# Attention scores by halves of the queries on quarters of the array, and one selection for four heads

## The chip, the cores and the metric

The kernel runs on one core of a Trainium2 chip. The metric is the time of the whole program on the device, in microseconds (us). The engines are TensorE (PE for matmuls, PEld for its weight loads), VectorE (DVE), ScalarE (ACT), GpSimd (POOL) and SyncE (SP, which issues most DMAs). Matmul results land in PSUM, which VectorE and ScalarE read.

## The reference

Three layers in a row, all in fp32: windowed attention, a layer of eight experts with a capacity, and a dense layer.

```python
# q, k, v: (4, 8, 576, 64); rel[i, j] = i - j; slopes: one per head
scores = scale * np.matmul(q, k.transpose(0, 1, 3, 2))
bias = slopes[:, None, None] * (-np.abs(rel))[None, :, :]
mask = (rel >= 0) & (rel < 128)
scores = np.where(mask, scores + bias[None], -1e9)
attn = softmax(scores)                     # over the keys
x = attn @ v                               # then (2304, 512)
# experts: each token goes to one of 8, at most 288 each, by logits in sorted order
out[mask_e] = np.maximum(x[mask_e] @ w1[e], 0) @ w2[e]
# dense: h = x @ w_in; (h * sigmoid(h)) @ w_out
```

A query sees the 128 keys that end with its own, so over a block of 128 queries it needs its own block of keys and the block before.

## The kernel before

The 2304 tokens are cut into 18 tiles of 128 queries (t = 0 to 17). The heads of a tile are done in two halves of four: the first half has heads 0, 1, 4, 5, the second 2, 3, 6, 7. Heads 0 to 3 lie on partitions 0 to 63 of the loaded q and k, heads 4 to 7 on partitions 64 to 127 (j = 0, 1 in the code), so that two heads can be multiplied at once on the two row halves of the array.

Each head of a tile goes through these steps. `scores` (L196) multiplies the 128 queries of a head with 256 keys, the block before and the tile's own, into PSUM. `softmax` first selects (L217): of the two keys that stand for the same place in the block, a query keeps the one that lies in its window (the older block's where key > query, the mask `older`), for two heads at a time; since exactly 128 keys remain, everything behind works on 128 columns. L221 adds the bias table (`tab`), scales, and takes the row maximum of one head. L213 on ScalarE takes the exponential of one head. `turn` transposes the four heads of a half on TensorE (L230), ScalarE copies them out of PSUM (L238; L245 for tiles with one key block), and GpSimd splits them back into the part of the older and of the own block (L239, L241). `values` (L271) multiplies these with v, 73 columns a head, on two column halves of the array; VectorE divides by the row sums (L274 to L286). `gate` (L252) multiplies the v of the next tile with the experts' weights, on four column strips; its transpose (L259) and copy (L260) put the result beside v. `first_choices` (L83 on TensorE, L73 and L76 on GpSimd) counts experts for the routing behind attention, and from tile 4 on ScalarE and GpSimd split early expert weights (L679, L680).

Tiles 0 and 9 start a sequence with nothing before it, and have one key block (`nb` is 1). Tiles 4 and 13 hold the end of one sequence and the start of the next.

The order on TensorE, ScalarE and GpSimd is written out by hand (`keep`, `keep_in_program_order`). One turn of the loop over t runs: transposes of the tile's first half; the values of the second half of the tile before; transposes of the second half; the scores of both halves of tile t + 1; its gate; the selections, maxima and exponentials of tile t + 1; the values of the first half of tile t. In turns 1 and 2 ScalarE also scales bias tables (L352) between the two halves' exponentials. On VectorE the selections and maxima are kept in order; the divisions are placed by the scheduler between them. Scores have two buffers per head pair in PSUM, so those of one tile are written while nothing of the tile before is still read. Loads of q, k and v (L124 to L135) run three tiles ahead on SyncE's queue.

Behind attention comes the routing, a chain of short steps on VectorE and TensorE (about 120 to 150 us), and then the two expert layers and the dense layer, dense matmuls to the end.

Of the kernel before, what the change touches and what calls it, by code (L numbers as in the profile page):

```python
# [8 lines left out]
F32 = mybir.dt.float32  # L9
# [3 lines left out]
I32 = mybir.dt.int32  # L13
AF = mybir.ActivationFunctionType
ALU = mybir.AluOpType
AX = mybir.AxisListType
PSUM = bass.MemoryType.PSUM
DRAM = bass.MemoryType.DRAM

P = 128  # L20
# [9 lines left out]
def attn_consts():  # L30

    q = np.arange(P)[:, None]
    k = np.arange(P)[None, :]
    far = np.where(q >= k, q - k, q + P - k)
    first = np.where(q >= k, far, MASKED)
    upper = np.where((q >= 64) & ((k < 64) | (k > q)), MASKED, far)
    after = np.where((k < 64) & (k > q), MASKED, far)
    return np.stack([first, far, upper, after, k > q], 1).astype(np.float32)  # L40


NJ = 319
# [3 lines left out]
def first_choices(tc, at, k, X0, t, gts, pgb, room):  # L47

    nc = tc.nc
    keep = tc.keep_in_program_order  # L50
    ident, grid = k.ident, k.grid
    m = at.tile([P, 1], F32, name="m", bufs=2)
    nc.vector.tensor_reduce(m, X0[:, t, :], AX.X, ALU.min)
    if t == 0:
        yield
        pm = pgb[0:1, 0:P]
        keep(nc.tensor.transpose(pm, m, ident))
        mr = at.tile([1, 2], F32, name="mr")
        nc.vector.tensor_reduce(mr[:, 0:1], pm, AX.X, ALU.max)
        nc.vector.tensor_reduce(mr[:, 1:2], pm, AX.X, ALU.min)  # L60
        ob = at.tile([1, P], F32, name="ob")
        nc.vector.memset(ob, 1.0)
        yield
        pb = pgb[:, P:P + 2]
        keep(nc.tensor.matmul(pb, ob, mr, start=True, stop=True))
        mb = at.tile([P, 2], F32, name="mb")
        nc.vector.tensor_copy(mb, pb)
        rg = at.tile([P, 1], F32, name="rg")
        nc.vector.tensor_tensor(rg, mb[:, 0:1], mb[:, 1:2], ALU.subtract)
        nc.vector.tensor_scalar(grid, grid, rg, mb[:, 1:2], ALU.mult, ALU.add)  # L70
    yield
    fb = at.tile([P, E], BF16, name="fb", bufs=2)
    keep(nc.gpsimd.tensor_scalar(fb, X0[:, t, :], m, None, ALU.is_le))  # L73
    gt = gts[t % 2]
    if t < NT - 2:
        keep(nc.gpsimd.tensor_scalar(gt[:, 0:NJ], grid, m, None, ALU.is_le))  # L76
    else:
        keep(nc.vector.tensor_scalar(gt[:, 0:NJ].rearrange("p (a b) -> p a b", b=29),
                                     grid.rearrange("p (a b) -> p a b", b=NJ), m, None, ALU.is_le))
    yield  # L80
    if t == NT - 1:
        k.busy(tc, room, 5)
    keep(nc.tensor.matmul(pgb[0:E, 0:NJ + 1], fb, gt, start=(t == 0), stop=(t == NT - 1)))  # L83
    yield
# [6 lines left out]
def attention(ctx, tc, qT, kT, vA, vT, wg, rel, k, xtab, X0, X, pgb, wts):  # L91


    nc = tc.nc
    ident = k.ident
    at = ctx.enter_context(tc.tile_pool(name="at", bufs=1))
    ps_s = ctx.enter_context(tc.tile_pool(name="ps_s", bufs=2, space=PSUM))
    ps_t = ctx.enter_context(tc.tile_pool(name="ps_t", bufs=1, space=PSUM))
    ps_o = ctx.enter_context(tc.tile_pool(name="ps_o", bufs=2, space=PSUM))

    tab = at.tile([P, H, 4, P], F32, name="tab")
    relt = at.tile([P, 5, P], F32, name="relt")
    older = relt[:, 4:5, :].bitcast(I32).to_broadcast([P, 2, P])
    wgb = at.tile([P, 4, 32], F32, name="wgb")
    nc.gpsimd.memset(wgb, 0.0)
    ks = at.tile([P, 4, 4, P], F32, name="ks")
    va = at.tile([P, VS, H, AUG], F32, name="va")

    gts = [at.tile([P, NJ + 1], BF16, name=f"gt{i}") for i in range(2)]
# [3 lines left out]
    def slope(h):  # L113
        return -8.0 * 2.0 ** (-(h + 1))

    qs, vts = {}, {}
# [20 lines left out]
    def heads(g):  # L137
        return [2 * g, 2 * g + 1, 2 * g + 4, 2 * g + 5]

    wz = at.tile([P, 512], BF16, name="wz")  # L140
    nc.vector.memset(wz, 0.0)

    def warm(n):
        for i in range(n):
            tc.keep_in_program_order(nc.tensor.matmul(pgb, wz[:, 0:P], wz, start=True, stop=True))

    warm(10)
    load(0)
    for j in range(2):
        nc.gpsimd.dma_start(wgb[64 * j:64 * j + 64, :, 8 * j:8 * j + 8],  # L150
# [3 lines left out]
    first = at.tile([1, 1], F32, name="first")  # L154
# [11 lines left out]
    keep = tc.keep_in_program_order  # L166
    tiles, halves, gates, last = {}, {}, {}, []
# [8 lines left out]

    def open_tile(t):

        sl, ps = t % 4, (t - 1) % 4
        nb = 1 if t in (0, 9) else 2  # L180
        first, st = (sl, 1) if nb == 1 else (min(ps, sl), abs(ps - sl))
        tiles[t] = dict(nb=nb, sl=sl, ps=ps, keys=slice(first, first + (nb - 1) * st + 1, st),
                        cur=0 if nb == 1 else int(ps < sl),
                        kind=0 if nb == 1 else 2 if t in (4, 13) else 3 if t in (5, 14) else 1)

    def scores(n):
        t, g = divmod(n, 2)
        if g == 0:
            open_tile(t)
        T = tiles[t]  # L190
        pss = [ps_s.tile([P, 2, 2, P], F32, name=f"pss{j}") for j in range(2)]
        for i in range(2):
            c = 2 * g + i
            for j in range(2):
                r = slice(64 * j, 64 * j + 64)
                keep(nc.tensor.matmul(pss[j][:, i, :T["nb"], :], qs[t][r, c, :], ks[r, T["keys"], c, :], start=True, stop=True))  # L196
        halves[n] = dict(pss=pss)

    def softmax(n):
        t, g = divmod(n, 2)  # L200
        T, pss = tiles[t], halves[n]["pss"]
        cur = T["cur"]
        sc = at.tile([P, 4, P], F32, name="sc", bufs=2)
        mx = at.tile([P, 4], F32, name="mx", bufs=4)
        pe = at.tile([P, 4, P], F32, name="pe", bufs=2)
        if n == 2:
            for h in range(H):
                keep(nc.vector.tensor_scalar_mul(tab[:, h, 1, :], relt[:, 1, :], slope(h)))
        follow = []

        def exp(*cs):
            for c in cs:
                keep(nc.scalar.activation(pe[:, c, :], sc[:, c, :], AF.Exp, bias=mx[:, c:c + 1], scale=-1.0))  # L213

        for j in range(2):
            if T["nb"] == 2:
                x = nc.vector.copy_predicated(pss[j][:, :, cur, :], older, pss[j][:, :, 1 - cur, :])  # L217
                follow.append(keep(x) if follow or n > 1 else x)
            for i in range(2):
                h, c = 2 * g + 4 * j + i, 2 * j + i  # L220
                x = nc.vector.tensor_tensor_reduce(sc[:, c, :], pss[j][:, i, cur, :], tab[:, h, T["kind"], :],  # L221
                                                   -0.125, 3.0e38, ALU.add, ALU.min, mx[:, c:c + 1])
                follow.append(keep(x) if follow or n > 1 else x)
        halves[n]["pe"], halves[n]["exp"] = pe, exp

    def turn(n):
# [37 lines left out]
    def values(n):  # L264
        t, g = divmod(n, 2)
        T, parts = tiles[t], halves[n]["parts"]
        po = T["po"][g][:, 0:4 * AUG].rearrange("p (h c) -> p h c", c=AUG)
        for c in range(4):
            for i, (w, s) in enumerate(parts):
                for r in (0, 64):  # L270
                    keep(nc.tensor.matmul(po[r:r + 64, c, :], w[:, c, r:r + 64], va[:, s, heads(g)[c], :],  # L271
                                          start=(i == 0), stop=(i == len(parts) - 1), tile_position=(0, r)))
        rs = at.tile([P, 4, 1], F32, name="rs", bufs=3)
        nc.vector.tensor_scalar_add(rs, po[:, :, 72:73], 1e-9)  # L274
        nc.vector.reciprocal(rs, rs)
        nc.vector.tensor_tensor(T["lg"][:, 4 * g:4 * g + 4, :], po[:, :, D:72], rs.to_broadcast([P, 4, E]), ALU.mult)

        def x():
            return nc.vector.tensor_tensor(
                T["xt"][:, :, 2 * g:2 * g + 2, :], po[:, :, 0:D].rearrange("p (a b) d -> p a b d", a=2),  # L280
                rs.rearrange("p (a b) d -> p a b d", a=2).to_broadcast([P, 2, 2, D]), ALU.mult)

        if n < 2 * NT - 1:
            x()
        if g == 1:
            nc.vector.tensor_reduce(X0[:, t, :], T["lg"].rearrange("p h e -> p e h"), AX.X, ALU.add, negate=True)  # L286
            if t < NT - 1:
                nc.sync.dma_start(xtab[t * P:(t + 1) * P, :], T["xt"].rearrange("p a b d -> p (a b d)"))
            if t == NT - 1:
                keep(nc.gpsimd.tensor_copy(X[:, t, :], X0[:, t, :]))  # L290
            counts[t] = first_choices(tc, at, k, X0, t, gts, pgb, halves[n]["pss"][0].rearrange("p a b c -> p (a b c)"))
            next(counts[t])
            if t == NT - 1:
                last.append(x)
# [4 lines left out]
    counts = {}  # L299
# [14 lines left out]
    for t in range(NT):  # L314
        a, b = 2 * t, 2 * t + 1
# [704 lines left out]
```

## Time and profile before

| what | us |
|---|---|
| median of 3 runs (lowest to highest) | 773.82 (772.61 to 774.51) |
| profiled execution | 773.07 |
| its span, first to last instruction | 771.0 |
| TensorE busy (share of the span) | 750.1 (97%) |
| VectorE busy | 433.9 (56%) |
| ScalarE busy | 323.1 (42%) |
| GpSimd busy | 125.7 (16%) |
| scores of tile 0 start, scores of tile 17 start | 5.64, 109.99 |

Busy times overlap between engines. TensorE's matmuls are pipelined, so that its busy time says that something was in flight, not that the array worked at its full rate. Shares of the whole span mix stages with different limits: attention takes the first 120 us, the dense matmuls from about 157 us on take the rest.

### The profile page before, as it was taken

The page shows a single profiled execution, that of the slowest core. Times are in us where ns is not written, and L with a number is a line of the kernel's source. Part 1 is how long each engine was busy: PE and PEld are TensorE (multiplying, and loading weights), DVE is VectorE, ACT ScalarE, POOL GpSimd, SP SyncE. Part 2 cuts the span into 40 slices and gives each one's busy share as a digit, 9 for nine tenths or more (in the row PEclk, how much of TensorE's full clock was granted, in tenths as well). Part 3 has the DMA queues.
Part 4 walks back from the last instruction along what each step waited for, and adds up shares of the span by engine and source line. Part 5 has one row for each costly group of instructions (what it writes and reads, how often), then busy time and mean ns, then how long its engine had stood idle before and what let it go on. Part 6 is the DMA issues. An engine that isn't in the chain of part 4 may idle for free.

```text
span 771.0 us, 13966 instructions
## 1 busy us (share of the span) xinstructions
PE 750.1 (97%) x5380; PEld 643.5 (83%) x5380; DVE 433.9 (56%) x1141; ACT 323.1 (42%) x665; POOL 125.7 (16%) x183
## 2 busy tenths in 40 slices
PE   8999999699999999999999999999999999999996
PEld 5777775399999989999888888888888888888895
DVE  6888886448899768776499633222422233222331
ACT  5677772046566546554355332221412232222322
POOL 2577871321022110000000002000100001000100
PEclk9999999799999999999999999999999999999999
DMA  8999840148798688676344011000100001000100
GB/s 238 279 317 285 270 151 28 34 116 263 237 306 269 212 278 275 217 225 220 103 148 137 1 54 55 1 0 1 57 26 1 1 0 56 1 0 1 42 14 27
DMA packets 38341, 95.36 MB, mean 124 GB/s; under 512 B 4576, under 2 KB 9984, under 8 KB 38272
## 3 DMA queue, kind: packets, MB, share of 16 engines
q1 hardware_dynamic: 35072, 84.72, 34.6%
q0 software_dynamic: 3040, 9.46, 3.7%
q8 instruction: 43, 0.70, 0.4%
q10 hardware_dynamic: 160, 0.26, 0.1%
q14 instruction: 26, 0.21, 0.1%
HBM read 80.27 MB, written 14.16 MB: 122 GB/s over the span
## 4 chain that ended last, share of the span: by engine, by line
PE 64%; DMA 7%; DVE 5%; issue 2%; ACT 2%; POOLq 0%; ACTq 0%
PE y L865 25%; PE p L799 6%; DMA raw<-w 6%; PE pt L719 4%; PE p L719 4%; PE pt L720 4%; PE p L720 4%; PE pt L718 4%; PE p L718 4%; PE y L719 2%; PE y L718 2%; PE y L720 2%; DVE w L691 2%; ACT w L690 1%; PE pt L783 1%
## 5 line engine op out<-in xcount | busy, mean ns | idle before, releaser
L865 PE MATMUL y<-w,gh 128*128 128x512 f32 x548 | 180.8, 389 | 0.0
L865 PEld LDWEIGHTS y<-w,gh 128*128 128x128 f32 x548 | 102.2, 188 | 20.5
L865 PE MATMUL y<-w,gl 128*128 128x512 f32 x274 | 106.7, 389 | 0.0
L691 DVE TENSOR_TENSOR w<-raw,w 128x1024 fp32r<-128x1024 f32 x59 | 72.1, 1222 | 36.2 <-ACT w L690 36.1
L877 POOL DMA_INDIRECT out<-raw,idx x18 | 17.4, 967 | 454.5 <-ACT raw L875 420.8
L799 PE MATMUL p<-xh,w 128*128 128x288 f32 x512 | 81.1, 297 | 1.7 <-DVE hl L803 1.6
L690 ACT CAST w<-raw 128x1024 fp32r<-128x1024 f32 x59 | 61.9, 1048 | 39.8 <-DMA raw<-w 22.5
L909 DVE TENSOR_TENSOR s<-pt,s 128x512 f32<-128x512 f32 (+1 forms) x40 | 25.5, 637 | 92.3 <-ACT s L908 92.3
L909 DVE TENSOR_TENSOR s<-p,s 128x512 f32<-128x512 f32 (+1 forms) x40 | 25.5, 637 | 91.4 <-ACT s L908 91.4
L719 PE MATMUL y<-hl,w 128*128 128x288 f32 x256 | 74.4, 296 | 0.0
L799 PEld LDWEIGHTS p<-xh,w 128*128 128x128 f32 x512 | 71.6, 188 | 3.1 <-DVE hl L803 2.4
L720 PE MATMUL y<-hh,w 128*128 128x288 f32 x256 | 73.8, 295 | 0.0
L919 DVE TENSOR_TENSOR gl<-s,gh 128x512 fp32r<-128x512 f32 (+1 forms) x73 | 48.0, 658 | 42.8 <-ACT gh L918 42.7
L718 PE MATMUL y<-hh,w 128*128 128x288 f32 x256 | 69.3, 299 | 0.0
L918 ACT CAST gh<-s 128x512 fp32r<-128x512 f32 (+1 forms) x73 | 43.4, 594 | 55.3 <-DVE s L909 38.3
L908 ACT ACTIVATE s<-pt 128x512 f32<-128x512 f32 (+1 forms) x40 | 22.2, 555 | 101.8 <-PE pt L720 97.2
L908 ACT ACTIVATE s<-p 128x512 f32<-128x512 f32 (+1 forms) x40 | 22.2, 555 | 98.6 <-PE p L720 93.9
L865 PEld LDWEIGHTS y<-w,gl 128*128 128x128 f32 x274 | 51.4, 188 | 10.7
L719 PE MATMUL pt<-yl,w 128*128 128x512 f32 (+1 forms) x160 | 58.8, 368 | 0.0
L718 PE MATMUL p<-yh,w 128*128 128x512 f32 (+1 forms) x160 | 58.8, 368 | 0.0
L718 PE MATMUL pt<-yh,w 128*128 128x512 f32 (+1 forms) x160 | 58.8, 368 | 0.0
L720 PE MATMUL pt<-yh,w 128*128 128x512 f32 (+1 forms) x160 | 58.8, 368 | 0.0
(189 smaller groups left out, 1491.0 us busy)
## 6 DMA issues: line engine op xcount, KB each, us to landing
raw<-w SPq DMA_DIRECT2D x96, 512.0 KB, 4.4
va<-vA SPq DMA_DIRECT2D x18, 292.0 KB, 5.1
ks<-kT SPq DMA_DIRECT2D x36, 128.0 KB, 4.5
vt<-vT SPq DMA_DIRECT2D x18, 256.0 KB, 4.0
xtab<-xt SPq DMA_DIRECT2D x18, 256.0 KB, 5.6
yd<-yo SPq DMA_DIRECT2D x8, 576.0 KB, 4.3
qs<-qT SPq DMA_DIRECT2D x34, 128.0 KB, 4.1
yr<-yd SPq DMA_DIRECT2D x4, 1024.0 KB
```

The source lines that it names most:

```text
L690: nc.scalar.copy(hi, r)
L691: nc.vector.tensor_tensor(lo, r, hi, ALU.subtract)
L718: nc.tensor.matmul(out, whi, xhi, start=start, stop=False)
L719: nc.tensor.matmul(out, whi, xlo, start=False, stop=False)
L720: nc.tensor.matmul(out, wlo, xhi, start=False, stop=stop)
L799: nc.tensor.matmul(p, w[:, dc * P:dc * P + P], x[:, dc, :], start=(i + dc == 0), stop=(i == 2 and dc == DC - 1))
L865: mm = nc.tensor.matmul(a, x[:, w], y[:, 512:], start=(f + i == 0), stop=(f == FC2 - 1 and i == 2))
L877: nc.gpsimd.indirect_dma_start(out, bass.IndirectOffsetOnAxis(ap=idx128[:, c:c + 1], axis=0), ob, None)
L908: nc.scalar.activation(s, p, AF.Sigmoid)
L909: nc.vector.tensor_tensor(s, p, s, ALU.mult)
L918: nc.scalar.copy(gh, s)
L919: nc.vector.tensor_tensor(gl, s, gh, ALU.subtract)
```

## The change

The scores of a tile are taken by halves of the queries (u = 0: queries 0 to 63, u = 1: 64 to 127) as well as by the two row halves of the array, so that each matmul uses a quarter of the array (64 rows, 64 columns), and only the 192 keys that a half of the queries can see are multiplied. Of the older block the first half of the queries takes all 128 keys, of the own block the first 64; the second half takes the own 128 and the last 64 of the older. Keys of the older block that need no choice are written to the places of the own block that the half of the queries does not use, so that the mask for the selection is now true only within the same half of keys and queries. The selection then runs over four heads at once. The PSUM room is two fixed tiles in place of two alternating buffers, of the same size, and four of the ten starting matmuls write them once, so that nothing unwritten is read.

```diff
-    return np.stack([first, far, upper, after, k > q], 1).astype(np.float32)
+    return np.stack([first, far, upper, after, (k > q) & (k // 64 == q // 64)], 1).astype(np.float32)
...
-    older = relt[:, 4:5, :].bitcast(I32).to_broadcast([P, 2, P])
+    older = relt[:, 4:5, :].bitcast(I32).to_broadcast([P, 4, P])
...
-    warm(10)
+    warm(6)
+    banks = [ps_s.tile([P, 2, 2, 4, 64], F32, name=f"pss{i}") for i in range(2)]
+    for z in banks:
+        for j in range(2):
+            warm(1, z[:, j].rearrange("p i s x -> p (i s x)"))
...
-        pss = [ps_s.tile([P, 2, 2, P], F32, name=f"pss{j}") for j in range(2)]
+        pss = banks[n % 2]
+        sl, ps, L, R = T["sl"], T["ps"], slice(0, 64), slice(64, 128)
         for i in range(2):
             c = 2 * g + i
-            for j in range(2):
-                r = slice(64 * j, 64 * j + 64)
-                keep(nc.tensor.matmul(pss[j][:, i, :T["nb"], :], qs[t][r, c, :], ks[r, T["keys"], c, :], start=True, stop=True))
+            if T["nb"] == 2:
+                parts = [[(slice(0, 4, 3), ps, slice(0, P)), (slice(2, 4), sl, slice(0, P))],
+                         [(slice(2, 3), sl, L), (slice(1, 2), ps, R)]]
+            else:
+                parts = [[(slice(2, 4), sl, slice(0, P))] * 2]
+            for two in parts:
+                for u, (o, s, x) in enumerate(two):
+                    for j in range(2):
+                        r, m = slice(64 * j, 64 * j + 64), slice(64 * u, 64 * u + 64)
+                        keep(nc.tensor.matmul(pss[m, j, i, o], qs[t][r, c, m], ks[r, s, c, x], start=True, stop=True,
+                                              tile_position=(64 * j, 64 * u)))
...
-        for j in range(2):
-            if T["nb"] == 2:
-                x = nc.vector.copy_predicated(pss[j][:, :, cur, :], older, pss[j][:, :, 1 - cur, :])
-                follow.append(keep(x) if follow or n > 1 else x)
-            for i in range(2):
-                h, c = 2 * g + 4 * j + i, 2 * j + i
-                x = nc.vector.tensor_tensor_reduce(sc[:, c, :], pss[j][:, i, cur, :], tab[:, h, T["kind"], :],
-                                                   -0.125, 3.0e38, ALU.add, ALU.min, mx[:, c:c + 1])
-                follow.append(keep(x) if follow or n > 1 else x)
+        w = pss.rearrange("p j i (b k) x -> p (j i) b (k x)", b=2)
+        if T["nb"] == 2:
+            x = nc.vector.copy_predicated(w[:, :, 1, :], older, w[:, :, 0, :])
+            follow.append(keep(x) if n > 1 else x)
+        for c in range(4):
+            h = 2 * g + 4 * (c // 2) + c % 2
+            x = nc.vector.tensor_tensor_reduce(sc[:, c, :], w[:, c, 1, :], tab[:, h, T["kind"], :],
+                                               -0.125, 3.0e38, ALU.add, ALU.min, mx[:, c:c + 1])
+            follow.append(keep(x) if follow or n > 1 else x)
```

## Rows read from the trace of the kernel before

**Rows 1.** Busy time by stretch:

```profile
core 0: us, PE busy (x) PEld busy (x) DVE busy (x) ACT busy (x) POOL busy (x), PEclk, DMA share, GB/s
30.70:61.50 30.80, 30.80 (x491) 24.24 (x490) 26.77 (x150) 21.02 (x62) 22.04 (x38) 1.00 0.99 308
...
120.90:156.60 35.70, 27.92 (x212) 15.88 (x212) 19.75 (x75) 2.28 (x5) 8.09 (x9) 0.86 0.12 34
```

**Rows 2.** Timeline of PE: start us, us, engine, line, operation, count:

```profile
79.21 2.00 PE L196 MATMUL pss<-ks,qs 64*128 64x256 f32 x16
...
82.82 0.60 PE L230 MATMUL pst<-cst,pe 128*128 128x128 f32 x4
83.38 0.35 PE L271 MATMUL po<-va,pp 128*64 128x73 f32 x4
83.53 0.33 PE L271 MATMUL po<-va,pc 128*64 128x73 f32 x4
83.66 0.33 PE L271 MATMUL po<-va,pp 128*64 128x73 f32 x4
...
85.37 2.00 PE L196 MATMUL pss<-ks,qs 64*128 64x256 f32 x16
```

**Rows 3.** Timeline of DVE, the same tile:

```profile
80.37 0.43 DVE L217 COPY_PREDICATED pss<-relt,pss 128x256 f32<-128x256 int32 x1 [0.29 <-PE pss L196]
80.84 0.29 DVE L221 CUSTOM_DVE_ANT_0 sc<-pss,tab 128x128 f32<-128x128 f32 x1
...
86.53 0.43 DVE L217 COPY_PREDICATED pss<-relt,pss 128x256 f32<-128x256 int32 x1 [0.29 <-PE pss L196]
```

**Rows 4.** Timeline of ACT, the same tile:

```profile
81.23 0.69 ACT L213 ACTIVATE pe<-sc,mx 128x128 f32<-128x128 f32 x2 [0.76 <-DVE mx L221]
...
82.06 0.69 ACT L213 ACTIVATE pe<-sc,mx 128x128 f32<-128x128 f32 x2
```

**Rows 5.** Timelines of PE and ACT, first and last of tile 10:

```profile
67.14 0.49 PE L196 MATMUL pss<-ks,qs 64*128 64x256 f32 x2
...
72.05 0.69 ACT L213 ACTIVATE pe<-sc,mx 128x128 f32<-128x128 f32 x2
72.79 0.33 PE L230 MATMUL pst<-cst,pe 128*128 128x128 f32 x1
73.05 0.49 PE L196 MATMUL pss<-ks,qs 64*128 64x256 f32 x2
```

**Rows 6.** Timeline of PE, up to 79.35 and up to 79.6: scores begun:

```profile
79.21 0.49 PE L196 MATMUL pss<-ks,qs 64*128 64x256 f32 x2
79.21 0.70 PE L196 MATMUL pss<-ks,qs 64*128 64x256 f32 x4
```

**Rows 7.** Timeline of PE at the gate's matmuls:

```profile
81.14 0.32 PE L252 MATMUL po<-vt,wgb 128*32 128x128 f32 x4
81.27 0.29 PE L252 MATMUL po<-vt,wgb 128*32 128x128 f32 x4
```

**Rows 8.** Groups by shape: count | busy us, mean ns | idle before, releaser:

```profile
L271 PE MATMUL po<-va,pc 128*64 128x73 f32 x512 | 34.5, 227 | 0.0
L217 DVE COPY_PREDICATED pss<-relt,pss 128x256 f32<-128x256 int32 x64 | 27.2, 426 | 5.2 <-PE pss L196 5.2
L909 DVE TENSOR_TENSOR s<-pt,s 128x512 f32<-128x512 f32 x32 | 22.1, 690 | 82.8 <-ACT s L908 82.8
L909 DVE TENSOR_TENSOR s<-p,s 128x256 f32<-128x256 f32 x8 | 3.4, 424 | 7.6 <-ACT s L908 7.6
L495 PE MATMUL pc<-ones,nC 128*8 128x1 bf16 x54 | 1.8, 163 | 0.0
```

**Rows 9.** Timeline of ACT in turn 1:

```profile
19.89 1.34 ACT L352 ACTIVATE tab<-relt 128x256 f32<-128x256 f32 x4
```

**Rows 10.** Timeline of SP, the keys of tile 13:

```profile
70.55 1.11 SPq L124 DMA_DIRECT2D ks<-kT  x2
```

**Rows 11.** Timeline of PE, counts in the routing:

```profile
124.76 0.59 PE L495 MATMUL pc<-ones,nC 128*8 128x1 bf16 x18
```

More of the change, by code (lines that the diff above doesn't have):

```diff
@@ L96, in attention @@
     at = ctx.enter_context(tc.tile_pool(name="at", bufs=1))
-    ps_s = ctx.enter_context(tc.tile_pool(name="ps_s", bufs=2, space=PSUM))
+    ps_s = ctx.enter_context(tc.tile_pool(name="ps_s", bufs=1, space=PSUM))
     ps_t = ctx.enter_context(tc.tile_pool(name="ps_t", bufs=1, space=PSUM))
@@ L141, in attention, with warm @@
     nc.vector.memset(wz, 0.0)
-    def warm(n):
+    def warm(n, out=pgb):
         for i in range(n):
-            tc.keep_in_program_order(nc.tensor.matmul(pgb, wz[:, 0:P], wz, start=True, stop=True))
-    warm(10)
+            tc.keep_in_program_order(nc.tensor.matmul(out, wz[:, 0:P], wz, start=True, stop=True))
+    warm(6)
[3 more added lines that the diff above has]
+            warm(1, z[:, j].rearrange("p i s x -> p (i s x)"))
     load(0)
@@ L177, in open_tile @@
     def open_tile(t):
-        sl, ps = t % 4, (t - 1) % 4
         nb = 1 if t in (0, 9) else 2
-        first, st = (sl, 1) if nb == 1 else (min(ps, sl), abs(ps - sl))
-        tiles[t] = dict(nb=nb, sl=sl, ps=ps, keys=slice(first, first + (nb - 1) * st + 1, st),
-                        cur=0 if nb == 1 else int(ps < sl),
+        tiles[t] = dict(nb=nb, sl=t % 4, ps=(t - 1) % 4,
                         kind=0 if nb == 1 else 2 if t in (4, 13) else 3 if t in (5, 14) else 1)
@@ L201, in softmax @@
         T, pss = tiles[t], halves[n]["pss"]
-        cur = T["cur"]
         sc = at.tile([P, 4, P], F32, name="sc", bufs=2)
@@ L290, in values @@
                 keep(nc.gpsimd.tensor_copy(X[:, t, :], X0[:, t, :]))
-            counts[t] = first_choices(tc, at, k, X0, t, gts, pgb, halves[n]["pss"][0].rearrange("p a b c -> p (a b c)"))
+            counts[t] = first_choices(tc, at, k, X0, t, gts, pgb, halves[n]["pss"][:, 0].rearrange("p i s x -> p (i s x)"))
             next(counts[t])
```

## Prediction, made before the change was run

> **What bounds the kernel now.** I read the busy times by stretch first, then the timelines of one tile on TensorE, VectorE and ScalarE, then the stretches in which TensorE has less to do. The change touches attention only, some 5 to 120 us of the 771.0 us span. In tiles 4 to 8 TensorE is busy in all of the 30.80 us, VectorE in 26.77 and ScalarE in 21.02, and the DMA engines are at 0.99 [rows 1]. In the steady state a tile's scores start at 79.21 us and those of the next at 85.37, so a tile takes 6.16 us [rows 2]; twelve tiles repeat this (scores of tiles 4 to 8 and 11 to 17).
>
> Which wait ends last? On TensorE one piece of work follows the other. VectorE begins a tile's selections at 80.37 and the next tile's at 86.53; ahead of the latter it waited 0.29 us for the scores, the only wait of note, so its work takes 5.87 [rows 3]. ScalarE waits 0.76 us for the first row maximum of a tile [rows 4]. So TensorE's own length sets the period, with two chains close behind. Tile 10 shows the nearest: tile 9 has one key block, so the two blocks of values within tile 10's period are half as long, 1 us less for TensorE; yet that period is 73.05 - 67.14 = 5.91 us [rows 5]. There ScalarE's last exponential ends at 72.74 and the transpose that needs it starts at 72.79. Less work on TensorE therefore pays only until a transpose waits for its exponential.
>
> **The scores on TensorE.** One fp32 matmul is two records (two passes). Now 16 records of 256 columns make a tile. Two records on different row halves of the array run together: two span 0.49 us, four 0.70 [rows 6], so a pair of passes costs 0.215 us, and eight of them 1.72. From 79.21 to the gate at 81.14 are 1.93 us [rows 2, 7]; of the 0.21 left I put half on the first weight load and half on the change to the gate's shape.
>
> After it, each head pair takes four quarter matmuls of 128 columns and four of 64, 64 records a tile. I take four quarters to run together: four column strips do (four records span 0.32 us, and the second four, which start at 81.27, 0.29 [rows 7]), two row halves do [rows 6], two column halves do [rows 2]; rows and columns split at once stand nowhere in this trace. A set of four passes then costs 0.108 us at 128 columns (half of 0.215). At 64 I take 0.056: the 73-column sets of two halves follow each other at half of 83.66 - 83.53 = 0.13 us [rows 2], 0.063, weights of 64 columns included. A head pair is 2 x 0.108 + 2 x 0.056 = 0.33 us, four make 1.32, and with a first load of 64 columns (0.05) and the change of shape (0.1) 1.47 us: 0.46 less per tile. Ends: two quarters at a time give 2.64 + 0.15 = 2.79, that is 0.86 more; a floor per record is the second rival.
>
> The first half of the heads is complete earlier too: the last of its passes starts at 0.05 + 0.66 - 0.06 = 0.65, lasts some 0.22 (a 73-column one 0.227 [rows 8]), and VectorE follows at about 0.93 us after the start of the scores (0.03 for the last of the four and 0.03 for the semaphore), not 1.16 [rows 2, 3].
>
> **The selection on VectorE.** Four selections of 256 elements (0.43 us; 0.47 from one's start to that of the next instruction [rows 3]) become two of 512. Of the other two-input rows, an addition over 256 elements takes as long as the selection, 0.424 to its 0.426, and one over 512 takes 0.690 [rows 8]. I take 0.69, and 0.735 to the next instruction; the upper end is 2 x 0.47 = 0.94 (nothing saved), and below 0.69 I see no row of this rate. That is 4 x 0.47 - 2 x 0.735 = 0.41 us less of VectorE's work per tile; VectorE isn't the bound, so by itself this is worth nothing. But the first maximum now waits for a selection of all four heads, 0.735 where it was 0.47.
>
> **What is late next.** From the start of a tile's scores to the last exponential of its first half, before: 1.16 (scores), 0.47 (selection), 0.39 (first maximum to ScalarE, 80.84 to 81.23), 1.52 (81.23 to 82.06 + 0.69), 3.54 in all [rows 3, 4]. After: 0.93 + 0.735 + 0.39 + 1.52 = 3.575, not earlier at all. The fourth transpose of the first half needs that exponential and starts 73.05 - 72.79 = 0.26 ahead of the next piece, or less where it does not wait [rows 5]; the next piece is the second half's values at 83.38, that is at 4.17 [rows 2]. So the transpose stands at 3.91 or later, with slack; 0.46 earlier it would stand at 3.45 to 3.5, and has to wait: until 3.575 + 0.05, which puts the values at 3.885. So a tile gains 0.285 us, not 0.46: about 5.87 us per tile. The other chains fit into that: second half's exponentials (5.91 as in tile 10, less 0.23 for the scores and 0.2 for the first half's selections, plus 0.27 for the longer selection of its own: 5.75), VectorE's work (5.87 - 0.41 = 5.46).
>
> Sum: twelve tiles at 0.285 make 3.4 us. Tiles 1 and 10, which hang on the second half's exponentials, gain 5.91 - 5.75, about 0.2 each, 0.4. Tiles 2 and 3 gain nothing: there ScalarE does 1.34 us of table scaling between the exponentials [rows 9], and everything behind it starts as late as before, since the first exponential does. Tiles 0 and 9 have one key block of 128, the same time in quarters. The four starting matmuls that now write the score banks are four of the ten that ran anyway; the banks alternate as the two buffers did, so no new wait for a free bank. In all 3.8 us. The loads hold: the keys of tile 13, scored at 85.37, were issued at 70.55 [rows 2, 10], and a pace faster by 5% leaves that; if the 0.99 of rows 1 were a limit for tiles 4 to 8, 1.4 us of the gain would go.
>
> What follows attention starts 3.8 us earlier and is otherwise the same: the profiled execution would go from 773.07 to 769.3, the median of three, which is 0.75 above it, from 773.8 to **770.0 us**.
>
> **Rivals.**
> *TensorE alone binds* (the first maximum comes 0.2 us sooner than I add up, and the exponentials are in time): 12 x 0.46 + 0.4 = 5.9 us, 767.9. For it: ScalarE and VectorE have slack in the sum of their work [rows 1]. Against: of the 3.575 only 0.93 and 0.735 are estimates, and each would have to be well too high.
>
> *A floor per record.* Eighteen small matmuls in one place of the array follow each other at (0.59 - 0.16) / 17 = 0.025 us, though each has one column [rows 8, 11]. If the 64-column quarters kept to that one after the other, a set of four would take 0.10, not 0.056: the first half is complete at 1.10, the last exponential of it at 3.75, and a tile gains 0.11 us, 1.3 us in all with tiles 1 and 10 at nothing: 772.5. Against it: four column strips lie within 0.03 us of each other [rows 7]. The Trainium skill ("TensorE: Matmul & The Clock Gate", section "Wait — 56ns, not 53.3ns?") says that start-to-start never drops below about 25 ns, however few the columns. Rows 11 agree with it, rows 7 don't where the strips differ; by it the time would be this rival's 772.5.
>
> *The merged selection saves nothing* (0.94): the last exponential of the first half at 3.78, gain 0.08 a tile, 1.0 us, 772.8. Its output and input lie in two banks, which no row here shows.
>
> *Slower: quarters don't run together four at a time.* Place: the scores of 16 tiles; price 0.86 us a tile, some 13 to 14 us, 787. It decides from where a set of four takes 1.35 times what one takes ((1.93 - 0.15) / 1.32); above that the scores are longer than now. For it: no row splits rows and columns at once, and 64 records with 64 loads in 1.3 us is one instruction in 10 ns, where the values' blocks have one in 16. Against: each split by itself runs together. The Trainium skill ("TensorE: Matmul & The Clock Gate", section "Measured speedup vs the span model") reports a speedup of 10.6 for sixteen tiles split both ways, by which this rival falls away; no run here shows it yet.
>
> *Half of it is given back behind attention.* The granted clock is 1.00 in tiles 4 to 8 and 0.86 on average over 120.9 to 156.6, where routing leaves TensorE less to do [rows 1]: part of that stretch runs at 1.2 GHz. If the time at the lower level ended where it ends now while the work came 3.8 us earlier, 3.8 us more of it would run at half speed and 1.9 us be lost: 771.9. One trace can't tell whether that stretch moves with the work.
>
> **How the numbers follow.** Forecast (the transpose waits) 0.45, TensorE alone 0.12, floor 0.12, merged selection saves nothing 0.08, lower clock 0.10, quarters not together 0.06; 0.07 for another order of VectorE's free instructions, to either side. A measurement of this kernel tells about 0.3% from no change, 2.3 us. Faster by more: the forecast, TensorE alone and small parts of the others, 0.58. Within: floor, selection, clock, 0.31. Slower: 0.11. The range takes in TensorE alone with another 0.6 us below and the two cases near 772.6 with 0.7 us above: 767.3 to 773.3; the 787 is left out.
>
> **What would show it.** Right: scores of a tile to the gate 1.45 to 1.55 us; 32 selections at 0.69; scores of one tile to those of the next 5.8 to 5.95; the first selection waiting for TensorE still, and the fourth transpose of the first half starting 0.05 after its exponential ends. TensorE alone: a period of 5.70 and no such wait. Floor: 64-column records 0.025 apart, scores 1.8. Wrong altogether: scores above 1.93, or loads that TensorE waits for in tiles 4 to 8, or a stretch behind attention that is longer by over 1 us.

## The result: undisturbed tiles are as short as forecast, and in others TensorE stands still

The changed kernel takes 779.64 us (median of 7 runs, 776.64 to 782.23) and the kernel before, measured beside it, 773.14 (7 runs, 771.67 to 774.94): a ratio of 1.0083 with a 95% interval of 1.0059 to 1.0107. The forecast was 770.0 us, a gain. The profiled execution took 782.23 us, its span 780.5; it is the slowest of the seven, so that it shows more of the loss (9.2 us above the profiled one of before) than the medians do (6.5). All of it lies in attention: the last values start at 128.27 us in place of 118.59, 9.7 us later, and from there to the end it is 652.2 us now and was 652.4.

The waits of TensorE, from tile 4 to the end of attention, show where it went. Columns: engine, tile and line, what ended the wait; total us, times, longest. First the kernel before, 30 to 120 us:

```profile
PE pst L230 <- ACT pt L238: 0.2, 1, 0.2
PE pgb L83 <- POOL gt L76: 0.2, 1, 0.2
```

The changed kernel, the same stretch:

```profile
PE po L281 <- issue: 6.0, 4, 2.4
PE pss L206 <- issue: 2.8, 1, 2.8
PE po L262 <- issue: 0.7, 1, 0.7
PE po L269 <- ACT gates L307: 0.4, 1, 0.4
```

"issue" means that TensorE waited for nothing that the profile shows: no data, no engine, no buffer. These waits fall inside pieces of work that have all they need. The longest, on the timeline of TensorE (start us, us, engine, line, operation, count, wait), splits one tile's scores, the next one a tile's values:

```profile
58.53 1.23 PE L206 MATMUL pss<-ks,qs 64*64 64x128 f32 x47
62.54 0.76 PE L206 MATMUL pss<-ks,qs 64*64 64x64 f32 x12 [2.79 <-issue]
...
102.39 0.29 PE L281 MATMUL po<-va,pc 128*64 128x73 f32 x3
105.05 0.22 PE L281 MATMUL po<-va,pc 128*64 128x73 f32 x1 [2.37 <-issue]
```

Tiles that no such wait hits are short. Scores, the gate behind them, and the next scores, then the selection on VectorE:

```profile
114.17 1.57 PE L206 MATMUL pss<-ks,qs 64*64 64x128 f32 x64
115.67 0.43 PE L262 MATMUL po<-vt,wgb 128*32 128x128 f32 x8
119.99 1.22 PE L206 MATMUL pss<-ks,qs 64*64 64x128 f32 x46
```

```profile
115.13 0.70 DVE L227 COPY_PREDICATED pss<-relt,pss 128x512 f32<-128x512 int32 x1 [0.23 <-PE pss L206]
115.86 0.29 DVE L231 CUSTOM_DVE_ANT_0 sc<-pss,tab 128x128 f32<-128x128 f32 x1
```

The tile takes 5.82 us where it took 6.16 [rows 2], its scores 1.50 up to the gate where they took 1.93 [rows 2, 7], and the selection 0.73 to the next instruction. The forecast had 5.87, 1.47 and 0.735.

**Where the waits fall.** Counted over all of TensorE's instructions in the trace, in order (matmuls, weight loads, and its own waits on semaphores), each of the long ones comes at a count that leaves 193 when divided by 256. The busy times by stretch show it too. Each of these stretches runs from the end of one such wait to the end of the next (columns as in [rows 1]; the counts of PE and PEld are what matters here):

```profile
37.50:48.28 10.78, 9.87 (x251) 8.06 (x252) 8.68 (x45) 5.86 (x18) 6.72 (x13) 1.00 0.87 265
48.28:54.29 6.01, 5.34 (x127) 4.35 (x126) 4.47 (x28) 3.51 (x11) 3.05 (x6) 1.00 0.95 295
54.29:62.53 8.24, 5.45 (x126) 4.47 (x127) 5.20 (x30) 4.74 (x14) 6.62 (x12) 1.00 0.96 286
...
105.04:111.05 6.01, 4.62 (x127) 3.81 (x126) 4.33 (x24) 2.55 (x7) 3.46 (x6) 1.00 0.72 213
```

Three of them hold 253 matmuls and loads (256 with three waits on semaphores), and the first 503 (512 with nine), twice that. A tile has some 293 (114.17 to 119.99 below), so the place within a tile moves; the count doesn't. The page lists a DMA queue of the kind instruction whose packets follow TensorE's count. Its row (packets, MB, share) in the page of before, and in that of after:

```profile
q8 instruction: 43, 0.70, 0.4%
```

```profile
q8 instruction: 49, 0.80, 0.4%
```

Each packet is 16 KB. TensorE's records went from 5380 matmuls and as many loads to 6180, 1600 instructions more, and six packets came with them: a packet is 256 instructions. In the longest wait one lies. DMA queues of the changed kernel at 57 to 59, 59 to 60 and 60 to 61 us (packets, MB, share of the 16 engines; a packet counts whole where it starts, so that a share can pass 100%):

```profile
q1 hardware_dynamic: 344, 0.69, 100.2%
...
q1 hardware_dynamic: 153, 0.26, 105.5%
q8 instruction: 1, 0.02, 6.6%
...
q1 hardware_dynamic: 145, 0.26, 99.7%
```

The packet starts at 60.00 us and has landed at 61.05; TensorE goes on at 62.54. It is the first since one that landed at 52.80. The data queue fills the engines all the while. So it is for each of the eight waits over 0.15 us at these counts: TensorE goes on 1.3 to 1.6 us after the packet has landed. Together the eight are 11.5 us long, 0.27 to 3.01 each, from one start to the next. In the kernel before, from 30 us to the end of attention, no packet landed less than 2.76 us ahead of the count at which TensorE passed on without a wait.

What is late is the packet's start, not its transfer. Of the 17 crossings from 30 us on, the eight with a wait had a packet that started 2.0 to 5.7 us after TensorE had passed the count before and took 1.1 to 1.5 us to land; at the other nine it started after 1.1 to 2.7 us and took 0.9 to 1.4. In the kernel before the packets start nearly as late (a median of 2.1 us, at most 4.1; 2.5 and 5.7 in the changed kernel), but there 256 instructions last longer (7.7 us in place of 5.2, table below). All of these are worked out from the trace.

**The sum of the loss.** 11.5 us of waits, and some 1.7 for 3.4 us at half the clock, which follow the 3 us in which TensorE stood (first row; the others are for later):

```profile
62.65:66.05 3.40, 3.40 (x57) 2.77 (x56) 1.63 (x9) 0.85 (x3) 0.64 (x1) 0.50 0.24 73
114.17:119.99 5.82, 5.82 (x147) 4.82 (x146) 5.13 (x29) 4.41 (x13) 5.07 (x9) 1.00 0.36 114
154.90:165.00 10.10, 6.02 (x37) 4.69 (x38) 2.03 (x4) 1.21 (x4) 5.80 (x7) 0.50 0.28 79
```

Less the 3.8 us of gain that was forecast, that makes 9.4 of the 9.7; with the 4.4 us of gain that e4 and e5 show below, it makes 8.8. The 1.7 is an estimate, half of 3.4.

### The profile page after: what moved, and what is told of

The parts are those of the page before. It is cut to its first block, busy times and chain, and to the rows that moved or that the text cites. A ratio compares the mean times of both kernels' runs of the same rounds, so it can differ in the third digit from the quotient of the medians.

```text
span 780.5 us, 15513 instructions
## 1 busy us (share of the span) xinstructions
PE 747.5 (96%) x6180; PEld 644.8 (83%) x6180; DVE 429.5 (55%) x1109; ACT 321.0 (41%) x665; POOL 127.0 (16%) x183
## 4 chain that ended last, share of the span: by engine, by line
PE 58%; DMA 9%; DVE 7%; ACT 2%; issue 2%; POOLq 0%; ACTq 0%; DVEq 0%
PE y L875 25%; DMA raw<-w 8%; PE pt L728 4%; PE p L728 4%; PE pt L729 4%; PE p L729 4%; PE pt L730 4%; PE p L730 4%; PE p L809 4%; DVE w L701 3%; ACT w L700 2%; PE y L728 1%; PE y L729 1%; PE y L730 1%; DVE bits L718 1%
```

## The theory and its rivals

*Supply.* TensorE's instructions come in packets of 256 through the same DMA engines as the data, about one packet ahead of their use (in the starts above, a packet starts only once TensorE has passed the count before the one that needs it). The change makes a tile some 94 instructions longer (293 in place of 199, by the counts of 114.17 to 119.99 above and of 79.21 to 85.37 in before, below) and 0.33 us shorter, so 256 of them last some 5 us in place of 8. With the DMA engines full, a packet can be later than that.

Rivals: the *quarters* hold TensorE up by their shape, or by many small records, whatever the DMAs do; the *merged selection* makes each half's first maximum later, and the loss comes from there; the *loads* of q and k themselves are late.

The runs came in three groups, each on one chip beside the kernel before. The ratios are those on record with the runs, and not the quotients of the two medians beside them:

| kernel | us | before beside it | ratio, 95% interval |
|---|---|---|---|
| two selections (e1) | 779.99 | 773.03 | 1.0081, 1.0053 to 1.0110 |
| merged selection alone (e2) | 772.56 | 773.03 | 0.9996, 0.9979 to 1.0012 |
| 192 keys in one piece (e3) | 774.94 | 773.03 | 1.0011, 0.9993 to 1.0030 |
| changed, fewer loads (e4) | 770.11 | 773.03 | 0.9965, 0.9949 to 0.9981 |
| before, fewer loads (e5) | 774.45 | 773.68 | 1.0000, 0.9979 to 1.0022 |
| before, idle instructions (e6) | 773.60 | 773.68 | 1.0000, 0.9982 to 1.0018 |
| ring of nine (e7) | 774.82 | 773.68 | 1.0023, 0.9997 to 1.0049 |
| ring of nine, loads moved (e8) | 774.60 | 773.68 | 1.0005, 0.9986 to 1.0024 |
| ring of nine, splits later (e9) | 772.73 | 774.16 | 0.9980, 0.9961 to 0.9999 |
| before, splits later (e10) | 773.29 | 774.16 | 0.9991, 0.9973 to 1.0009 |
| full width, four pieces (e11) | 803.50 | 774.16 | 1.0370, 1.0331 to 1.0409 |
| e11 with fewer loads (e12) | 803.59 | 774.16 | 1.0370, 1.0329 to 1.0410 |

## The selection, undone and alone

```diff
-        if T["nb"] == 2:
-            x = nc.vector.copy_predicated(w[:, :, 1, :], older, w[:, :, 0, :])
...
+            if T["nb"] == 2 and c % 2 == 0:
+                x = nc.vector.copy_predicated(w[:, c:c + 2, 1, :], older, w[:, c:c + 2, 0, :])
```

> The changed kernel with the merged selection undone: two selections of two heads each in a half, as before; the scores stay in quarters. Supply theory (TensorE's instructions come in packets of 16 KB, 256 of them, and the 96 more per tile make TensorE wait at the packets' boundaries): the number of TensorE's instructions is that of the changed kernel, so waits of 1 to 3 us on TensorE remain at the scores and values in tiles 4 to 15, and the time is 777 to 783 us. Rival, the merged selection (a first maximum that comes 0.27 us later in each half): the loss goes, 768 to 773 us.

779.99 us, the changed kernel's time, with its waits (30 to 120 us):

```profile
PE po L281 <- issue: 5.1, 4, 2.5
PE pss L206 <- issue: 1.7, 1, 1.7
PE po L262 <- issue: 1.0, 1, 1.0
```

The other way round, the kernel before with full-width scores and one selection for four heads:

```diff
-        pss = [ps_s.tile([P, 2, 2, P], F32, name=f"pss{j}") for j in range(2)]
+        pss = ps_s.tile([P, 2, 2, 2, P], F32, name="pss")
...
+        w = pss.rearrange("p j i b x -> p (j i) b x")
+            x = nc.vector.copy_predicated(w[:, :, cur, :], older, w[:, :, 1 - cur, :])
```

> The kernel before with the merged selection alone: full-width scores of 256 keys, one selection for four heads. Supply theory: TensorE's instructions are those of before, no wait of over 1 us on TensorE at the scores, 772 to 774.5 us. Rival, the merged selection: 0.27 to 0.5 us more per tile, 776 to 781 us.

772.56 us, no difference to before; no wait for issue on TensorE in tiles 4 to 17, and a tile takes 6.16 us as before (scores at 37.57, 43.73, 49.89). The rival of the merged selection falls, and so does its saving as a source of time: it is worth nothing while TensorE is the bound, as the prediction had it.

## The loads, taken from both kernels

```diff
     def load(t):
+        if t > 3:
+            qs[t] = qs[t - 1]
+            return
```

> The changed kernel without the loads of q and k from tile 4 on (the scores of those tiles use the q and k that are there, so that they are other scores; every instruction of the engines stays): about a third less is loaded during attention. Supply theory: an instruction packet that finds the DMA engines free lands sooner, the waits of 1 to 3 us on TensorE go or shrink below 0.5, 768 to 772 us. Rival (the number or shape of the instructions holds TensorE up, with the DMAs idle too): the waits stay, 778 to 782 us.

> The kernel before without the loads of q and k from tile 4 on (the scores of those tiles use the q and k that are there, so that they are other scores), as the control to the changed kernel without these loads. Supply theory: the instruction packets of before come in time anyway, 772 to 774 us, within 0.2% of before. Rival (the loads hold both kernels up as data): it gains as the changed kernel did, some 9 us, 762 to 766 us.

The changed kernel falls to 770.11 us, the kernel before stays (774.45, ratio 1.0000). All matmuls and weight loads are there, as many and in the same shapes; only the DMA engines have less to do. TensorE's waits from 30 us to the end of attention are then (e4):

```profile
PE po L272 <- ACT gates L310: 0.4, 1, 0.4
PE pgb L83 <- POOL gt L76: 0.3, 1, 0.3
```

and the busy times of tiles 4 to 8, which answer to [rows 1], first e4 and then the changed kernel:

```profile
30.82:59.95 29.13, 29.13 (x731) 24.13 (x730) 25.58 (x141) 20.48 (x62) 21.97 (x38) 1.00 0.62 193
```

```profile
31.44:62.54 31.10, 25.34 (x632) 20.80 (x632) 22.79 (x124) 17.99 (x53) 20.32 (x36) 1.00 0.94 284
```

With the DMA engines at 0.62 TensorE is busy throughout and takes 29.13 us for the five tiles, 5.83 each. With 0.94 it is busy for 25.34 of 31.10 and isn't through. The quarters as such hold nothing up: that rival falls. That the loads of q and k are late as data falls too, since before gains nothing without them, and no wait of TensorE in the changed kernel from 30 us on names a load. One of the counted waits over 0.15 us is left, of 0.18. Packets start sooner: a median of 1.25 us after TensorE passed the count before, at most 3.45, where it was 2.5 and 5.7. Attention ends at 114.62 us in e4 and at 119.01 in e5, so without the traffic the change is worth 4.4 us there; the forecast for it was 3.8. Against the changed kernel (128.27) it ends 13.65 us earlier, where the waits and the stretch at half clock add up to 13.2. The whole program gains less (0.9965 of before, 2.7 us): from the last values to the end e4's profile has 654.8 us and that of before 652.4. The profiles of before with fewer loads (e5) and with nothing changed (e6) have 657.8 and 653.8 there, though their code behind attention is that of before, so that such differences are not shown to be the change's.

What the chain does in such a tile, on TensorE and ScalarE (e4):

```profile
42.47 1.57 PE L209 MATMUL pss<-ks,qs 64*64 64x128 f32 x64
43.97 0.42 PE L265 MATMUL po<-vt,wgb 128*32 128x128 f32 x8
...
45.66 0.73 PE L243 MATMUL pst<-cst,pe 128*128 128x128 f32 x4
46.31 0.35 PE L284 MATMUL po<-va,pp 128*64 128x73 f32 x4
...
48.30 1.57 PE L209 MATMUL pss<-ks,qs 64*64 64x128 f32 x64
```

```profile
44.56 0.69 ACT L226 ACTIVATE pe<-sc,mx 128x128 f32<-128x128 f32 x2 [1.34 <-DVE mx L234]
...
45.31 0.69 ACT L226 ACTIVATE pe<-sc,mx 128x128 f32<-128x128 f32 x2
```

The last exponential of the first half ends at 46.00, 3.53 us behind the start of the scores (forecast 3.575). The fourth transpose waits for it and starts at 46.06 (read from the trace, record by record): the four span 0.73 us here, 0.60 where none waits [rows 2]. The values of the second half follow at 3.84 (forecast 3.885).

## Fewer instructions

In three tiles of four the 192 keys of a quarter can be taken by one matmul, if the keys are kept as half blocks of 64 in a ring; the array's columns stay the same.

```diff
-    ks = at.tile([P, 4, 4, P], F32, name="ks")
+    ks = at.tile([P, 8, 4, 64], F32, name="ks")
...
+        elif sl:
+            parts = [[(slice(0, 3), slice(ps, ps + 3)), (slice(1, 4), slice(ps + 1, ps + 4))]]
```

> The changed kernel with the 192 keys of a quarter taken by one matmul where they lie side by side (the keys are kept as half blocks of 64 in a ring of eight; tiles whose own block lies at the ring's start still take two): the scores of such a tile are 32 records in place of 64, some 230 instructions per tile in place of 292, with the same columns in the array. Supply theory: 256 instructions last some 6.4 us and the packets come in time in most tiles; tiles of 5.7 to 5.9 us, waits at few boundaries, 769 to 774 us. Rival (quarters themselves hold TensorE up, by their shape): the waits stay with the quarters, 778 us or more.

774.94 us, 5 us less than the changed kernel and a little above the upper end of the expectation (774). The waits for issue from 30 us on (TensorE's own, e3):

```profile
PE po L283 <- issue: 1.8, 1, 1.8
...
PE pst L242 <- issue: 0.9, 1, 0.9
```

By the count there are five over 0.15 us, 4.2 in all, still at 193 of 256. Fewer instructions, fewer waits, in the same quarters. They are not gone, since 256 instructions last 6.0 us here (the median) and single packets start up to 6.4 us after the 256 before them were begun.

With a ring of nine tiles, no tile is left that takes its keys in two pieces (shown against e3):

```diff
-    ks = at.tile([P, 8, 4, 64], F32, name="ks")
+    ks = at.tile([P, 18, 4, 64], F32, name="ks")
```

> As the one-piece kernel, with a ring of 18 half blocks for the keys (nine tiles), so that a tile's three half blocks lie side by side in every tile: 32 records for the scores in each, 228 instructions a tile. Supply theory: the tiles that kept two pieces (4, 8, 12, 16) no longer bring a block of 256 instructions that lasts under 6 us; fewer waits at boundaries than with the one-piece kernel, 771 to 774 us. Rival (the waits left there come from single long delays of a packet, whatever the pace): no change against it, 774 to 776 us.

774.82 us: no change, as the rival had it, but not by its cause. Of the counted waits one is left (1.46 us). In its place stands another, on ScalarE:

```profile
53.54 0.62 ACT L688 CAST w<-raw 128x512 fp32r<-128x512 f32 x1 [3.58 <-DMA raw<-w]
54.07 0.69 ACT L222 ACTIVATE pe<-sc,mx 128x128 f32<-128x128 f32 x2
54.66 0.24 ACT L306 COPY gates<-po 128x128 f32<-128x128 f32 x1
```

and on TensorE, which needs the copy of the gate:

```profile
54.96 0.33 PE L268 MATMUL po<-cst,gates 128*128 128x128 f32 x1 [2.69 <-ACT gates L306]
```

The splitting of the early expert weights stands ahead of the exponentials in ScalarE's order by hand. Its load was issued at 47.59 us and the split waits for it until 53.54. Neither before nor e3 has such a wait.

Next, on top of e7, the constants of the routing and the early expert weights are loaded later (e8):

```diff
-        if t == 6:
+        if t == 14:
             k.fetch(tc, at)
...
-EARLY = range(4, 14)
+EARLY = range(6, 16)
```

> As the kernel with the ring of nine, with two loads moved away from the tiles in which the DMA engines are full: the routing's constants (337 KB) are loaded in turn 14 in place of turn 6, and the five early expert weights (512 KB each) two turns later. Supply theory: the packets of tiles 5 to 9 land sooner, fewer waits of TensorE there, 769 to 772 us. Rival (the delay of a packet doesn't hang on how much is loaded): no change against the ring of nine. A loss would have to come from behind attention, where the weights are split later.

774.60 us, again no change. No counted wait over 0.15 us is left. Attention's last values come at 116.56 us, 2.0 earlier than in before, but ScalarE still waits 2.46 us once for such weights (until 74.94), and from the last values to the end it is 656.4 us where it was 652.4. That what was moved to later is missed there is not shown: each of these is one profile, and e7, which moves no load, has 655.2 there, e5 657.8.

Then, on top of e7 again, the constants alone are loaded later, and ScalarE splits the weights a turn later (e9; e10 is the kernel before with these two moves):

```diff
-        if t - 2 in EARLY:
-            wts.split_early(t - 2 - EARLY[0])
+        if t - 3 in EARLY:
+            wts.split_early(t - 3 - EARLY[0])
```

> As the kernel with the ring of nine, with the splitting of the early expert weights one turn later (two turns behind their load, since ScalarE waited 3.58 us for such a load ahead of the exponentials there) and the routing's constants (337 KB) loaded in turn 14 in place of turn 6. Theory (what the one-piece kernels still lose is one late load in front of ScalarE's exponentials, and few instruction packets): no wait of ScalarE for the weights over 0.5 us, tiles of 5.7 to 5.9 us, 769 to 772 us. Rival (other waits come up in its place): 773 to 776 us.

> The kernel before with the same two moves (weights split one turn later, constants loaded in turn 14), as the control. By either theory no change, 772.5 to 774.5 us: ScalarE has no such wait in before.

e9 takes 772.73 us beside 774.16 for before: 0.9980 (0.9961 to 0.9999), above the 769 to 772 that was expected. By its ratio it is the fastest of the kernels that load everything (e2, on another chip, has 772.56 us at 0.9996); the interval ends just below 1, and before with the same two moves (773.29) isn't told apart from either. ScalarE waits for no weights any more; tiles take 5.81 us from 31.96 to 49.39, and counted waits of 1.2 us are left in two places. What takes the rest is not shown. The longest waits of TensorE from 30 us on (e9) are one ahead of tile 4 (until 29.85 us), one of the two counted ones, and one for a load of v, in the tiles about the start of the second sequence (until 67.97):

```profile
PE po L280 <- ACT va L269: 1.1, 1, 1.1
PE po L280 <- issue: 0.7, 1, 0.7
PE pss L205 <- DMA va<-vA: 0.6, 1, 0.6
```

## Instructions added without quarters

To add instructions to the kernel before, 12 that do nothing were put behind each of its score matmuls.

```diff
                 keep(nc.tensor.matmul(pss[j][:, i, :T["nb"], :], qs[t][r, c, :], ks[r, T["keys"], c, :], start=True, stop=True))
+                if T["nb"] == 2:
+                    for _ in range(12):
+                        keep(nc.tensor.nop(nofuse=True))
```

> The kernel before, with full-width scores of 256 keys and two selections a half, and 12 instructions that do nothing behind each score matmul, 96 per tile with two key blocks, about as many as the quarters add. Supply theory: every 256 instructions last some 6 us or less, TensorE waits 1 to 3 us at such boundaries in tiles 4 to 15, 777 to 785 us. Rival (quarters by their shape hold TensorE up, or one such instruction costs only its own issue, 96 x 0.01 to 0.03 us a tile where it isn't hidden): no such waits, and a time of at most 775 us if they are hidden, or evenly longer tiles if they are not.

773.60 us, no change, but the page has the 43 packets of before: the instructions never became part of the program. The run says nothing about the theory, and is one more run of before in effect.

The other way is to cut the full-width scores into four pieces of 64 keys, which gives as many records as the changed kernel has.

```diff
-                keep(nc.tensor.matmul(pss[j][:, i, :T["nb"], :], qs[t][r, c, :], ks[r, T["keys"], c, :], start=True, stop=True))
+                    keep(nc.tensor.matmul(pss[j][:, i, x // 2, o], qs[t][r, c, :], ks[r, e, c, o], start=True, stop=True))
```

> The kernel before with the scores at full width, each 256 keys in four pieces of 64: 64 records of scores per tile, as many instructions as the changed kernel has, and no quarter of the array; selections as before. Supply theory: TensorE waits 1 to 3 us at boundaries of 256 instructions in tiles 4 to 15, as in the changed kernel; 779 to 790 us. Rival (quarters of the array hold TensorE up): no such waits, and a time above before only by what longer scores cost, evenly in every tile.

> The kernel with full-width scores in four pieces, without the loads of q and k from tile 4 on (the scores of those tiles use the q and k that are there, so that they are other scores). Supply theory: the waits at boundaries go, 5 to 10 us less than with the loads; what is left above before is the array's own time for the pieces. Rival (the pieces themselves cost the time): as with the loads, within 2 us.

803.50 us with the loads and 803.59 without, and hardly a wait for issue: the expectation of the supply theory was wrong here. The reason is in the scores (e11, TensorE, then its weight loads):

```profile
88.52 3.79 PE L198 MATMUL pss<-ks,qs 64*128 64x64 f32 x64
92.24 0.43 PE L254 MATMUL po<-vt,wgb 128*32 128x128 f32 x8
```

```profile
88.52 3.65 PEld L198 LDWEIGHTS pss<-ks,qs 64*128 64x128 f32 x64
```

Each piece loads 128 columns of weights again, 0.057 us each, one behind the other; the tile grows to 7.95 us, and 256 instructions last 6.8 us (the median). One wait over 1 us is left with the loads (1.3 us by the profile) and none without:

```profile
PE po L273 <- issue: 1.3, 1, 1.3
```

So the number of instructions alone doesn't cost; what the runs point to is their number per microsecond. The kernels in a line, each from one profiled execution (how long 256 of TensorE's instructions last, the median from 30 us to the end of attention, less the waits; the DMA share at 30 to 90 us; and the waits over 0.15 us at the count of 193, worked out from the trace):

| kernel | 256 instructions last, us | DMA share | waits: times, us in all |
|---|---|---|---|
| before | 7.7 | 0.93 | none |
| e11 | 6.8 | 0.78 | 2, 1.7 |
| e12 | 6.9 | 0.50 | none |
| e7 | 6.5 | 0.95 | 1, 1.5 |
| e8 | 6.4 | 0.95 | none |
| e9 | 6.4 | 0.93 | 2, 1.2 |
| e3 | 6.0 | 0.93 | 5, 4.2 |
| e1 | 5.2 | 0.90 | 7, 9.6 |
| changed | 5.2 | 0.87 | 8, 11.5 |
| e4 | 5.2 | 0.64 | 1, 0.2 |

Both causes are needed: longer blocks take most of the waits away, and so does a lighter load of the DMA engines. No run adds instructions at an unchanged pace of the rest, so apart from the changed kernel and e4 the line rests on kernels that differ in more than one thing. What makes a packet start late (its place behind data, or the moment at which it is asked for) wasn't tried.

## Why the prediction was wrong, step by step

*Scores on TensorE:* right. Quarters run four at a time; 1.50 us for 1.47. The slower rival falls. The floor per record falls too: it would have made the scores 1.8 us.

*Selection:* right, 0.70 and 0.73 us. The first half is complete at 0.96 us (115.13 - 114.17), for 0.93.

*What is late next:* right. The fourth transpose waits for its exponential; 5.82 and 5.83 us a tile for 5.87. The exponentials come 0.04 us earlier than added up, which is the difference. TensorE alone would have given 5.70.

*The loads hold:* this is the step that failed. It looked at the keys of one tile, found them issued 15 us ahead, and took the DMA share of 0.99 at worst as a limit to the pace of the data, worth 1.4 us. It left out that TensorE's instructions are a load as well, on the same engines, with one packet ahead and no 15 us. The prediction even worked out the density, "one instruction in 10 ns", and used it only to ask whether the array can run four quarters at once. What it needed was at hand: the page of before lists the instruction queue with 43 packets and 0.70 MB; with 5380 matmuls and as many loads that is some 250 instructions to a packet. A tile of before has 199 in 6.16 us, so one packet in 7.9 us:

```profile
79.21:85.37 6.16, 6.16 (x100) 4.85 (x99) 5.38 (x31) 4.49 (x13) 5.18 (x9) 1.00 0.73 229
```

With 96 more in 5.87 us it is one in 5.1. With the engines at 0.99 [rows 1] and loads that take 4.5 to 5.0 us from issue to landing there (medians by queue listing, 30 to 62 us), a price of some us had to stand there as a rival at least: on the path, since nothing covers TensorE's own standstill.

The Trainium skill ("Runtime: NRT & Kernel Launch", section "Instruction fetch mechanics") says that the sequencer fetches the next block of 256 instructions through its own DMA queue while the current one runs, and that crossing a block is mostly hidden. The blocks of 16 KB agree with the row of the queue. "Mostly hidden" holds for before; in the changed kernel eight crossings cost 11.5 us.

*What follows attention is the same:* right, 652.2 and 652.4 us. The rival of a clock that stays down until a fixed time falls: the stretch at half clock in the routing (154.90 to 165.00 above) lay 8.8 us earlier in before, where attention ended 9.7 us earlier, with the same length and level:

```profile
146.10:156.20 10.10, 6.28 (x34) 4.65 (x35) 1.50 (x4) 1.61 (x4) 5.39 (x7) 0.50 0.31 85
```

Its length isn't fixed: by the granted clock in the traces it is 13.7 us in e6, the same program as before, and 17.1 in e5. A dip that the prediction didn't have came instead, at 62.65 us, behind 3 us without work on TensorE.

*The chances:* the 0.11 for slower stood mainly for quarters that don't run together. The mechanism that came was among none of the rivals, though "loads that TensorE waits for in tiles 4 to 8" stood among what would prove it wrong.

## What to carry to other kernels

An edit that splits one matmul into several can be paid twice: in the array, and in instructions, which come through the DMA engines in packets. Before splitting, divide 256 by the new number of instructions per microsecond and set that beside the time that a load takes from issue to landing in the same stretch (here 7.7 us beside 4.5 to 5.0 had no wait, 5.2 had eight; a rule of thumb from these runs, not tested by itself); where the DMA engines are full and the two come near each other, take the split that needs fewer instructions (here one strided matmul of 192 keys in place of two), or thin out the loads. And a kernel made faster in one place asks for all its loads sooner: the next wait (here the early weights in front of ScalarE) is looked for before the gain is counted.

## What the runs showed of the hardware that was not expected

- TensorE stood for 0.3 to 3.0 us, with all its data there, at eight of 17 counts of 256 instructions, where a packet of instructions was late; it went on 1.3 to 1.6 us after the packet had landed. The profile calls such waits "issue".
- Four quarters of the array (64 rows, 64 columns) run together: 64 records of 128 and 64 columns with 64 loads in 1.50 us, 0.023 us a record.
- With 64 columns of data and 128 columns of weights a matmul, on two row halves of the array, the weight loads filled the time: 64 loads took 3.65 of the 3.72 us that 64 matmuls took up to the gate (e11).
- 3 us without work on TensorE was followed by 3.4 us at a granted clock of 0.50, the lower of its two levels.
